# A single-core decode block with a cached attention and a gated FFN: fewer PE instructions, larger weight chunks, one store, no block

## The chip, the cores and the metric

The kernel runs on 1 core of one Trainium2 chip. Its time is the device time of one execution in microseconds (us). "The span" is what the profile covers of one execution; it is 1.2 to 2.1 us shorter than the time, and that difference will matter. The page writes PE for the matmul engine, PEld for its weight loads, DVE for the vector engine, ACT for the scalar engine, SP for the engine whose queue issues most transfers, "landing" for the arrival of a transfer, and "L575" for line 575 of the kernel that was run.

## The reference

Two tokens (batch 2, one position each) pass through an adaLN-conditioned block: attention over the last 1024 keys of a cache with 32 heads of 192, then a gated FFN.

```python
mod = (_silu(c) @ w_mod).reshape(2, 6, 1, 640)          # w_mod: 640 x 3840
h = layernorm(x) * (1 + ca) + sa
q = (h @ wq)                                             # wq: 640 x 6144
scores = einsum('bhqd,bhkd->bhqk', q, k_cache[:, :, -1024:]) * 192 ** -0.5
o = einsum('bhqk,bhkd->bhqd', softmax(scores), v_cache[:, :, -1024:])
x = x + ga * (o.reshape(2, 1, 6144) @ wo)                # wo: 6144 x 640
h = layernorm(x) * (1 + cb) + sb
x = x + gb * ((gelu(h @ w_gate) * (h @ w_up)) @ w_down)  # 640 x 1536, 640 x 1536, 1536 x 640
```

Everything is bf16. Weights and the used part of the cache are 76.9 MB, and each byte is used for two rows at most.

## The kernel before

All large loads go out from SP in the order in which they are used: w_mod, wq, then K and V of 16 groups (4 heads of one batch row, 32 partitions a head, 32 keys a partition), wo, w_gate, w_up, w_down. wq, K, V and wo pass through a ring of 8 slots.

The parts that the change touches (cuts marked):

```python
KPS = SLOT // NQ                      # wq: one k per ring slot, 5 loads
...                                   # wo: 9 tiles per slot, 6 loads
WD_SPLIT = [(0, 2), (2, 1), (3, 1)]   # w_down: 6, 3 and 3 of 12 row blocks

# scores of one group: DVE multiplies K by q (prod), PE adds up over d with an identity
o_ap = ps[:, bk, ci * JC * GC:(ci + 1) * JC * GC].rearrange("p (j c) -> p j c", c=GC)
for t in range(NCH):                  # GC = 16, NCH = 12: 12 matmuls of 256 columns
    last = e.matmul(o_ap, lhsT=ident_b[:, :], rhs=prod[:, pz, :, t * GC:(t + 1) * GC], ...)

# FFN gate and up: the weights are the stationary operand, 60 matmuls of 2 columns each
for fc in range(FC):
    a, r = divmod(fc, FR)
    for k in range(KT):
        last = e.matmul(ps[:, bk, fc * 2:fc * 2 + 2],
                        lhsT=wv[:, k, a * P * FR:(a + 1) * P * FR].rearrange("p (m r) -> p m r", r=FR)[:, :, r],
                        rhs=h2T[:, k, :], start=(k == 0), stop=(k == KT - 1))
...
# the store, two transfers, and the block that holds the engines' programs
for b in range(B):
    S.dma(("sp", "act")[b], k_dma(out[b, 0, :]..., finb[b:P:32, :]), sem_out[b], ...)
with nc.Block() as block:
    @block.sync
    def _(e):
        S.emit("sp", e, tail=sp_tail)
    ...
```

## Time and profile before

Time before: 192.12 us median of 3 runs (191.79 to 192.21).

| | before |
|---|---|
| span of the profiled run | 190.5 us |
| DMA stream | 76.9 MB, 9 tenths busy from the second to the 38th of 40 slices |
| PE, DVE busy | 57%, 47% |
| last weight piece landed | 186.8 us |
| output ready, end of the span | 188.1 us, 190.5 us |
| PE instructions (matmuls and weight loads) | 2802 |

From the page of the kernel before: its engines, the row of DMA busy tenths and the rate in 40 slices, three DMA queues (packets, MB, share of the 16 engines' time), and the start of the chain that ended last.

```profile
PE 109.4 (57%) x1401; PEld 74.3 (39%) x1401; DVE 88.7 (47%) x147; ACT 29.2 (15%) x74; POOL 3.0 (2%) x14
DMA  7999999999999999999999999999999999999960
GB/s 259 388 416 441 423 427 428 418 436 426 418 429 426 421 427 425 421 428 424 423 426 431 418 423 434 419 421 431 428 416 434 420 423 424 426 421 432 399 252 8
DMA packets 7234, 77.09 MB, mean 405 GB/s; under 512 B 818, under 2 KB 820, under 8 KB 1460
q1 hardware_dynamic: 7192, 76.88, 96.0%
q8 instruction: 11, 0.18, 0.4%
q14 instruction: 3, 0.02, 0.0%
DMA 71%; DVE 13%; SPq 5%; PE 4%; issue 3%; ACT 2%
```

The reader is to see that the DMA engines never rest before the 39th slice, and that the 39th (181.0 to 185.7 us) moves only 252 GB/s, though the last landing is yet to come: the 16 engines do not finish together. The small queue q8, "instruction", moved 11 packets of 16 KB between 26.0 and 187 us. I read them as blocks of PE's program that are fetched while the kernel runs; the experiments below show that their number goes with that of the PE instructions (9, 10 and 11 packets for 2334, 2590 and 2846).

The chain of waits of the kernel before in order of time, its last pieces (start in us, duration in us, what):

```profile
156.72 30.05 DMA r<-in_B_w_down_dram
186.77 0.04 issue
186.81 0.60 PE ps L625 x12
187.41 0.02 issue
187.44 0.33 DVE fin L630
187.77 0.02 issue
187.80 0.32 DVE finb L632
```

So the end is: a last landing at 186.77 us, 12 matmuls, two DVE instructions, then the store and the exit up to 190.5 us. The timeline of the FFN before (start, duration, engine, line, operation, operands; in brackets the idle time before and what ended it):

```profile
178.24 1.81 PE L605 MATMUL ps<-h2T,r 128*128 128x2 bf16 x60 [0.28 <-DVE h2T L376]
181.79 1.81 PE L605 MATMUL ps<-h2T,r 128*128 128x2 bf16 x60 [1.73 <-DMA r<-in_B_w_up_dram]
183.71 0.18 DVE L616 TENSOR_TENSOR aT<-ps,gl 128x24 bf16<-128x24 f32 x1 [5.53 <-PE ps L605]
```

**When each engine lands.** For each of the 49 weight and cache loads of the kernel before, all of 128 partitions, the trace records 16 increments of the load's semaphore (a counter that engines wait on), each with its time; the page counts 16 DMA engines. I read each increment as the finish of one engine. No trace shows this, as the increments don't name the engine; "an engine is late" stands below for "an increment is late". Sorted, they then show how far apart the engines are. For some transfers of the kernel before: time of the first increment, the 16 delays behind it in us, and how many packets of the instruction queue had gone before:

```
first at    delays of the 16 increments                                                    packets so far
 14.28   0.00 0.01 0.02 0.03 0.06 0.07 0.08 0.10 0.20 0.23 0.34 0.40 0.45 0.46 0.50 0.73    0
 28.99   0.00 0.04 0.05 0.06 0.09 0.10 0.12 0.13 0.25 0.36 0.43 0.47 0.48 0.52 0.74 1.78    1
 58.49   0.00 0.04 0.06 0.08 0.09 0.10 0.12 0.14 0.28 0.36 0.43 0.49 0.53 0.73 1.80 2.06    2
164.56   0.00 0.03 0.05 0.27 0.72 0.74 0.83 1.50 1.54 1.55 1.69 1.76 1.89 1.95 2.10 2.12    8
168.06   0.00 0.01 0.02 0.28 0.69 0.73 0.84 1.48 1.52 1.53 1.67 1.86 1.92 2.08 2.12 3.29    9
183.13   0.00 0.06 0.10 0.28 0.73 0.76 0.85 1.50 1.52 1.57 1.67 1.89 1.95 2.10 3.30 3.64   10
```

Packets of the instruction queue q8 started at 26.0, 56.7, 70.0, 88.4, 104.9, 121.1, 139.8, 158.1, 167.2, 181.3 and 185.9 us and took about 1.06 us each. After each of the first eight, one more engine stands about 1.5 us behind, which is more than the packet itself took (why is open), and it stays there: the DMA share is 1.01 in each of the windows from 40 to 160 us that I asked for, which leaves no idle time for catching up. One late engine of the table is not q8's: a second instruction queue, q14, moved an 8 KB packet (0.33 us) at 75.6 us, after which an engine is about 1.0 us later and stands over 1.3 us behind. So the row at 164.56 us has nine late engines after eight packets. The ninth and tenth packets of q8 make an engine late that was late already. These two engines, alone, set the landing at 186.77 us: the other fourteen had landed by 185.23.

### The profile page before, as it was taken

What the parts mean: (1) busy time and instruction counts of PE and PEld (TensorE: products, weight loads), DVE (VectorE), ACT (ScalarE), POOL (GpSimd) and SP (SyncE); (2) the same over time, 40 slices, a digit from 0 to 9 for tenths busy, and PEclk for the clock granted to TensorE, in tenths of its full rate; (3) what the DMA queues carried; (4) which work ended last, traced back from release to release, by engine and by line L of the source; (5) the groups of instructions that cost most, each with busy time, mean ns of one, the idle gap of its engine ahead of it and who ended that gap; (6) DMA issues with size and microseconds to landing.
All of it is one profiled execution on the core that took longest, in us unless ns stands there. A gap on an engine that the chain in (4) does not pass through costs nothing.

```text
span 190.5 us, 3243 instructions
## 1 busy us (share of the span) xinstructions
PE 109.4 (57%) x1401; PEld 74.3 (39%) x1401; DVE 88.7 (47%) x147; ACT 29.2 (15%) x74; POOL 3.0 (2%) x14
## 2 busy tenths in 40 slices
PE   0014853628678773674689656646759856224452
PEld 0011310105556552462457444434536624223450
DVE  6123000248699549458477476485495620003201
ACT  3031100370022101011011011012010230003400
POOL 6000000000000000000000000000000000000000
PEclk9999999999999999999957999999975995555555
DMA  7999999999999999999999999999999999999960
GB/s 259 388 416 441 423 427 428 418 436 426 418 429 426 421 427 425 421 428 424 423 426 431 418 423 434 419 421 431 428 416 434 420 423 424 426 421 432 399 252 8
DMA packets 7234, 77.09 MB, mean 405 GB/s; under 512 B 818, under 2 KB 820, under 8 KB 1460
## 3 DMA queue, kind: packets, MB, share of 16 engines
q1 hardware_dynamic: 7192, 76.88, 96.0%
q8 instruction: 11, 0.18, 0.4%
q14 instruction: 3, 0.02, 0.0%
q10 hardware_dynamic: 28, 0.01, 0.0%
HBM read 76.88 MB, written 0.00 MB: 404 GB/s over the span
## 4 chain that ended last, share of the span: by engine, by line
DMA 71%; DVE 13%; SPq 5%; PE 4%; issue 3%; ACT 2%
DMA ring<-in_A_k_cache_dram 39%; DMA ring<-in_A_wq_dram 16%; DMA r<-in_B_w_down_dram 16%; DVE prod L441 8%; SPq L246 5%; PE ps L454 3%; DVE S_sb L461 2%; ACT qbc L433 2%; PE ps L416 1%; DVE ps L436 1%; DVE M L464 1%; PE ps L480 0%; DVE rden L516 0%; PE ps L625 0%; DVE Sb_sb L486 0%
## 5 line engine op out<-in xcount | busy, mean ns | idle before, releaser
L441 DVE TENSOR_TENSOR prod<-ring,qbc 128x3072 bf16<-128x3072 bf16 x32 | 55.9, 1752 | 21.7 <-DMA ring<-in_A_k_cache_dram 21.7
L454 PE MATMUL ps<-prod,ident_b 128*128 128x256 bf16 x384 | 53.4, 296 | 21.0 <-DVE prod L441 21.0
L454 PEld LDWEIGHTS ps<-prod,ident_b 128*128 128x128 bf16 x384 | 38.2, 105 | 33.1 <-DVE prod L441 25.4
L518 ACT ACTIVATE On<-ps,rden 128x384 bf16<-128x384 f32 x16 | 9.3, 580 | 46.5 <-DVE rden L516 33.1
L480 PE MATMUL ps<-nmx,ones_f 1*128 1x4 f32 x32 | 6.5, 271 | 15.2 <-DVE nmx L471 15.2
L506 PE MATMUL ps<-ring,E_sb 128*8 128x384 bf16 x256 | 13.6, 334 | 0.0
L489 ACT ACTIVATE E_sb<-Sb_sb 128x128 bf16<-128x128 f32 x16 | 5.0, 309 | 53.3 <-DVE Sb_sb L486 53.3
L480 PEld LDWEIGHTS ps<-nmx,ones_f 1*128 1x128 f32 x32 | 5.1, 198 | 20.3 <-DVE nmx L471 20.3
L575 PE MATMUL ps<-ring,oT 128*2 128x160 bf16 x192 | 7.2, 333 | 8.3 <-DMA ring<-in_A_wo_dram 7.8
L461 DVE TENSOR_REDUCE S_sb<-ps 128x32 f32<-128x512 f32 x16 | 10.8, 673 | 1.7 <-PE ps L454 1.7
L416 PE MATMUL ps<-ring,hT 128*2 128x384 bf16 x80 | 7.1, 516 | 7.5 <-DMA ring<-in_A_wq_dram 6.7
L486 DVE TENSOR_TENSOR Sb_sb<-S_sb,ps 128x128 f32<-128x128 f32 x16 | 4.6, 288 | 10.7 <-PE ps L481 10.7
L575 PEld LDWEIGHTS ps<-ring,oT 128*2 128x2 bf16 x192 | 5.4, 115 | 9.9 <-DMA ring<-in_A_wo_dram 9.3
L592 DVE TENSOR_TENSOR lnt<-ps,modR 128x160 f32<-128x160 f32 x1 | 0.3, 324 | 17.5 <-PE ps L575 17.5
L345 PE MATMUL ps<-st,selstat 128*128 128x2 f32 x4 | 1.1, 349 | 11.2 <-ACT sqj L341 11.2
L427 DVE CAST qrow<-ps 128x384 bf16<-128x384 f32 x2 | 1.0, 553 | 13.7 <-PE ps L416 13.7
L416 PEld LDWEIGHTS ps<-ring,hT 128*2 128x2 bf16 x80 | 2.1, 108 | 12.6 <-DMA ring<-in_A_wq_dram 8.9
L530 PEld LDWEIGHTS ps<-On,zsel 128*128 128x128 bf16 x128 | 6.1, 110 | 1.2 <-ACT On L518 1.2
L530 PE MATMUL ps<-On,zsel 128*128 128x48 bf16 x128 | 6.0, 187 | 0.8 <-ACT On L518 0.8
L506 PEld LDWEIGHTS ps<-ring,E_sb 128*8 128x8 bf16 x256 | 4.9, 86 | 3.0 <-issue 0.5
L495 PEld LDWEIGHTS ps<-denp,maskc 128*128 128x128 f32 x32 | 5.3, 209 | 1.2 <-ACT E_sb L489 1.0
L396 PE MATMUL ps<-r,scT 128*2 128x480 bf16 x40 | 4.3, 596 | 2.1 <-DMA r<-in_w_mod_dram 2.1
(71 smaller groups left out, 74.9 us busy)
## 6 DMA issues: line engine op xcount, KB each, us to landing
ring<-in_A_k_cache_dram SPq DMA_DIRECT2D x16, 1536.0 KB, 25.1
ring<-in_A_v_cache_dram SPq DMA_DIRECT2D x16, 1536.0 KB, 25.6
ring<-in_A_wq_dram SPq DMA_DIRECT2D x5, 1536.0 KB, 23.9
ring<-in_A_wo_dram SPq DMA_DIRECT2D x5, 1440.0 KB, 24.7
r<-in_w_mod_dram SPq DMA_DIRECT2D x1, 4800.0 KB, 14.2
r<-in_B_w_gate_dram SPq DMA_DIRECT2D x1, 1920.0 KB, 26.9
r<-in_B_w_up_dram SPq DMA_DIRECT2D x1, 1920.0 KB, 31.0
r<-in_B_w_down_dram SPq DMA_DIRECT2D x1, 960.0 KB, 33.3
```

Of the source, the lines that this page charges most:

```text
L246: return lambda e: e.dma_start(dst, src)
L416: last = e.matmul(ps[32 * i:32 * i + B, n, 0:QW].rearrange("p (q d) -> p q d", d=Dh), lhsT=hT[:, k, :], rhs=wv[:, 2 * n:2 * n + 2, i, :], ...
L441: S.op("dve", lambda e: e.tensor_tensor(out=prod[:, 2 * (g % 2) + ci, :, :], in0=ring[:, sl, ci * JC * Dh:(ci + 1) * JC * Dh].rearrange("p ...
L454: last = e.matmul(o_ap, lhsT=ident_b[:, :], rhs=prod[:, pz, :, t * GC:(t + 1) * GC], start=(ci == 0 and t == 0), stop=(t == NCH - 1), skip ...
L461: S.op("dve", lambda e: e.tensor_reduce(out=S_sb[:, z, :], in_=ps[:, z, :].rearrange("p (j c) -> p j c", c=GC), axis=AX.X, op=ALU.add), re ...
L480: e.matmul(o_ap, lhsT=ones_f[0:1, :], rhs=nmx[:, z, :], start=True, stop=False)
L489: S.op("act", lambda e: e.activation(out=E_sb[:, z, :, :], in_=Sb_sb[:, z, :, :], func=ACTF.Exp, scale=SCALE, accum_out=denp[:, z:z + 1]), ...
L495: S.op("pe", lambda e: e.matmul(ps[:, BK_T, P + 16:P + 17], lhsT=maskc[:, :], rhs=denp[:, z:z + 1], start=True, stop=True), reads=[("denp" ...
L506: last = e.matmul(ps[32 * i:32 * i + 2 * HQ, BK_O, 0:ON], lhsT=E_sb[:, z, 2 * jp:2 * jp + 2, :].rearrange("p j h -> p (j h)"), rhs=ring[:, ...
L518: S.op("act", lambda e: e.activation(out=On[:, z, :], in_=ps[:, BK_O, 0:ON], func=ACTF.Identity, scale=rden[:, z:z + 1]), reads=[bank(BK_O ...
L530: last = e.matmul(ps[:, BK_OT, b * NT:(b + 1) * NT], lhsT=zsel[:, jj, x:x + P], rhs=On[:, z, jj * Dh + dd * NT:jj * Dh + (dd + 1) * NT], s ...
L575: last = e.matmul(ps[32 * i:32 * i + B, BK_M, 0:DR], lhsT=oT[:, t, :], rhs=wv[:, tl, i, :], start=(t == 0), stop=(t == NT - 1), tile_posit ...
```

## The change

Its stated intent: a third fewer PE instructions by wider sums and by letting the FFN weights be the moving operand, large wq and wo chunks, small last w_down pieces, one store, no block. The diff, cut to its core:

```diff
-    GC = 512 // J
+    GC = 512 // JC                       # sums: 6 matmuls of 512 columns in place of 12 of 256
-    KPS = SLOT // NQ                      # wq in 5, wo in 6 loads
-    ...
-    WD_SPLIT = [(0, 2), (2, 1), (3, 1)]
+    WQ_SPLIT = [(0, 2), (2, 3)]
+    WO_SPLIT = [(0, 28), (28, 17), (45, 3)]
+    WU_SPLIT = [(0, 3), (3, 2)]
+    WD_SPLIT = [(9, 3), (0, 5), (5, 3), (8, 1)]
...
-                e.matmul(o_ap, lhsT=ones_f[0:1, :], rhs=nmx[:, z, :], start=True, stop=False)
-                return e.matmul(o_ap, lhsT=ident_b[:, :], rhs=mneg[:, :], start=False, stop=True)
+            S.op("pe", lambda e: e.matmul(ps[:, BK_T, P:P + HQ], lhsT=bcL[:, :], rhs=bcR[:, z, :], ...
...                                        # sel: both batch rows in one matmul of 96 columns
-        def ffn_gu(bk, wv, key):           # 60 matmuls, weights stationary
+        def ffn_gu(bk, wv, name, splits):  # 20 matmuls, weights moving, four column groups
+                        wk = wv[:, k, :].rearrange("p (m i r) -> p i m r", i=NR, r=FR)
+                        for i in range(NR):
+                            last = e.matmul(ps[32 * i:32 * i + B, bk, 0:FT]..., lhsT=h2T[:, k, :],
+                                            rhs=wk[:, i, :, :], ..., tile_position=(0, 32 * i))
+        def a_T(e):                        # and 12 matmuls that transpose the result
...
-        for b in range(B):
-            S.dma(("sp", "act")[b], ...    # two stores
-        with nc.Block() as block:
-            ...
+        S.dma("sp", k_dma(out[:, 0, :].rearrange("b (i n) -> i b n", i=NR), finb[0:P:RB, :]),
+              sem_out, reads=["finb"], name="st_out")
+        S.resolve()                        # drops waits that other waits imply
+        S.emit("sp", nc.sync, tail=lambda e: e.wait_ge(sem_out, 16))
+        S.emit("pool", nc.gpsimd)
+        ...
```

The heads of a group are also no longer neighbours in memory, which lets q be read in unbroken columns of wq.

## The prediction

> **What bounds the kernel now.** The DMA stream. The page's slices show the 16 engines at 9 tenths busy from the second slice to the 38th, 416 to 441 GB/s, for 76.9 MB; PE is busy 57%, DVE 47%. The chain of waits is DMA for 71% and ends with the last w_down piece landing at 186.8 us, then 0.6 us of matmuls, 0.65 us of DVE, then 2.4 us of store and exit. So only three things count: bytes per engine, the slowest engine's finish, and what follows it. A faster PE in the attention loop is worth nothing by itself (the loop's DVE and PE wait for K).
>
> **The slowest engine.** The trace's semaphore records give 16 increments per DMA[...]. For the first loads they come within 0.73 us. For the last w_down piece: fourteen within 2.1 us of the first (183.1 to 185.2 us), two at 186.4 and 186.8 us. The instruction queue moved 11 packets of 16 KB, about 1.06 us each, and after nearly each of them one more engine is late by about 1.1 us for good. The first eight fall on different engines; the ninth (167 us) and tenth (181 us) on engines that are late already. Those two set the end. [...] 2802 PE instructions (1401 matmuls, 1401 loads) are 10.9 blocks.
>
> **What the change does.**
> - PE falls to about 1039 matmuls by my count, 2078 instructions, 8.1 blocks. Eight fetches, none doubled: last landing about 1.5 us earlier (183.1 + 2.1). This is the main gain.
> - Last w_down piece 4 matmuls instead of 12: about -0.2 us.
> - One store, no block: before, finished output to end is 2.4 us, with two stores landing at 189.8 and 190.1 us and an exit after; about -0.5 us.
> - Fewer, larger wq and wo packets (40 fewer per engine, net): rates of 12 KB and 15 KB rows differ by 0.2%, so about -0.15 us.
> - Costs off the path: queries ready about 2.3 us later (36 matmuls after the last wq landing, at 4 per 0.43 us); S reduction reads twice as much (0.67 to about 1.15 us), so DVE takes about 6.1 us a group against the stream's 7.4: it catches up by about 90 us. The ring stays issued some 10 us ahead, so no DMA gap.
> - Tail: gate and up each 5 rounds of 384 columns (about 1.65 us against 1.81), then a new transpose (12 matmuls, a copy, about 0.7 us). wo's last pieces end near 173.2 us, as before, h2T near 178.2, aT near 183.1, first down pieces done near 184.5 us, just ahead of the last landings. Little slack.
>
> **Predicted:** 192.1 - 2.5 = 189.6 us; 80% range 188.4 to 191.0. Faster by over 2%: 0.12; within 2%: 0.85; slower by over 2%: 0.03.
>
> **Right if:** the instruction queue shows 8 packets; the last landing is near 185.2 us with no engine over 2.2 us behind the first; DMA stays at 9 tenths, mean rate up about 1%; about 1.8 us from output ready to end; PE busy drops by some 20 us or more with nothing to show for it in the loop.
>
> **Wrong if:** the fetches still double up on an engine; the strided moving reads of gate and up (runs of 3 elements) run at half speed, which makes the tail compute-bound and costs 2 to 3 us; the late wq release or large wo pieces open a gap in the DMA row; or the head spread of K rows changes the rate.

The four gains in the list come to 2.35 us (1.5 + 0.2 + 0.5 + 0.15), put down as 2.5. A "block", here and in the expectations, is 256 PE instructions. The trace of the kernel before has 11 packets for 2802 PE instructions, 255 a packet, and in the experiments 256 instructions more were one packet more. That each increment is one engine's is the reading given above.

## The result

| | before | after |
|---|---|---|
| time, median | 192.06 us (191.79 to 192.21, 4 runs) | 188.92 us (188.76 to 189.1, 4 runs) |
| ratio | 1 | 0.9838, 95% interval 0.9821 to 0.9855 |
| span of the profiled run | 190.5 us | 187.6 us |
| time minus span in that run | 1.7 us | 1.3 us |
| last weight piece landed | 186.77 us | 184.75 us |
| span's end after output ready | 2.4 us | 1.8 us |

A ratio is the mean time of one kernel's runs over that of the other's of the same rounds, so it is not quite the ratio of the medians quoted. Executions over 1.5% slower than the fastest of the same kernel are left out of the means. The kernel is 1.6% faster, correct, and inside the predicted range, on its fast side.

The same lines of the page after the change:

```profile
PE 107.5 (57%) x1039; PEld 51.1 (27%) x1039; DVE 98.2 (52%) x147; ACT 29.9 (16%) x72; POOL 5.1 (3%) x23
DMA  7999998999999999999999999999999999999991
GB/s 254 402 451 435 430 459 372 422 435 424 430 422 422 427 425 426 427 424 420 419 432 432 422 423 422 421 438 422 424 423 422 419 488 428 416 384 442 398 396 45
DMA packets 6518, 77.03 MB, mean 411 GB/s; under 512 B 746, under 2 KB 876, under 8 KB 1516
q1 hardware_dynamic: 6492, 76.88, 97.1%
q8 instruction: 8, 0.13, 0.3%
q14 instruction: 2, 0.02, 0.0%
DMA 71%; DVE 15%; PE 7%; ACT 2%; SPq 2%; issue 1%
```

Bytes are the same and the DMA engines are as busy as before. The 39th slices (396 GB/s against 252) cannot be compared, as this one ends at 182.9 us, before any engine has finished; from 178.2 to 182.9 us the kernel before moved 392 GB/s too. What differs at the end is shown by the increments below. The instruction queue moved 8 packets in place of 11. PE is still busy 57%: the sums move the same columns through the array in half as many instructions (109.4 us of PE before, 107.5 after). Only the weight loads fell (74.3 to 51.1 us).

The end of the chain of waits and the FFN in the timeline, after the change:

```profile
152.72 31.64 DMA r<-in_B_w_down_dram
184.37 0.04 issue
184.41 0.72 PE ps L684 x16
185.13 0.02 issue
185.16 0.34 DVE fin L689
185.49 0.02 issue
185.52 0.32 DVE finb L691
```

```profile
175.51 1.89 PE L655 MATMUL ps<-r,h2T 128*2 128x384 bf16 x20 [0.28 <-DVE h2T L427]
180.10 0.86 PE L655 MATMUL ps<-r,h2T 128*2 128x384 bf16 x8 [0.70 <-DMA r<-in_B_w_up_dram]
181.70 0.47 PE L672 MATMUL ps<-selg,aR 128*128 128x2 bf16 x12 [0.74 <-DVE aR L664]
182.21 0.20 DVE L676 CAST aT<-ps 128x24 bf16<-128x24 f32 x1 [0.57 <-PE ps L672]
```

The gate takes as long as before (1.89 us against 1.81), the transpose and its copy take 0.7 us more, and still the tail waits for DMA. The FFN starts 2.7 us earlier than before, of which part is a higher granted clock of this run (see "The tail" below). The chain names the landing before the last one, that of the three-row piece at 184.37; the one-row piece landed at 184.75, and its matmuls are the last 4 of the 16.

The increments of the last w_down piece after the change, beside those before:

```
         first at    delays of the 16 increments
before   183.13   0.00 0.06 0.10 0.28 0.73 0.76 0.85 1.50 1.52 1.57 1.67 1.89 1.95 2.10 3.30 3.64
after    182.92   0.00 0.02 0.05 0.07 0.09 0.18 0.46 0.71 0.92 1.45 1.48 1.53 1.61 1.63 1.65 1.83
```

The first engine lands 0.21 us earlier, the last 2.02 us earlier. So nine tenths of the gain at the last landing came from the slowest engines, and one tenth from the stream's rate. Of the 8 packets, seven left an engine late; the eighth came at 182.8 us, when the first engine was about to finish.

**Two theories.** Mine: each 16 KB block of PE instructions that is fetched puts one DMA engine back for good; eight blocks fall on different engines, the ninth and tenth on engines already late; cutting PE instructions to about eight blocks takes those two away (about 1.5 us), and the rest of the gain comes from chunks, store and exit. The rival: the number of PE instructions as such is irrelevant; the larger chunks, the smaller last pieces or the lighter PE load do it, and the late engines are an accident of the run.

### The profile page after: what moved, and what is told of

Read it like the earlier page. It is cut to its first block, busy times and chain, and to the rows that moved or that the text cites. A ratio compares the mean times of both kernels' runs of the same rounds, so it can differ in the third digit from the quotient of the medians.

```text
span 187.6 us, 2409 instructions
## 1 busy us (share of the span) xinstructions
PE 107.5 (57%) x1039; PEld 51.1 (27%) x1039; DVE 98.2 (52%) x147; ACT 29.9 (16%) x72; POOL 5.1 (3%) x23
## 3 DMA queue, kind: packets, MB, share of 16 engines
q1 hardware_dynamic: 6492, 76.88, 97.1%
## 4 chain that ended last, share of the span: by engine, by line
DMA 71%; DVE 15%; PE 7%; ACT 2%; SPq 2%; issue 1%
DMA ring<-in_A_k_cache_dram 37%; DMA ring<-in_A_wq_dram 17%; DMA r<-in_B_w_down_dram 17%; DVE prod L490 9%; PE ps L502 4%; DVE S_sb L509 4%; PE ps L467 2%; SPq L266 2%; ACT qbc L483 2%; DVE ps L485 1%; DVE M L512 1%; ACT qrow L474 1%; PE ps L526 0%; DVE bcR L519 0%; PE ps L684 0%
## 5 line engine op out<-in xcount | busy, mean ns | idle before, releaser
L502 PE MATMUL ps<-prod,ident_b 128*128 128x512 bf16 x192 | 52.9, 419 | 14.4 <-DVE prod L490 14.4
L502 PEld LDWEIGHTS ps<-prod,ident_b 128*128 128x128 bf16 x192 | 17.5, 104 | 40.2 <-DVE prod L490 17.5
L509 DVE TENSOR_REDUCE S_sb<-ps 128x32 f32<-128x1024 f32 x16 | 19.3, 1206 | 2.1 <-PE ps L502 2.1
L526 PE MATMUL ps<-bcR,bcL 5*128 5x4 f32 x32 | 6.1, 258 | 21.9 <-DVE bcR L519 21.9
L467 PE MATMUL ps<-ring,hT 128*2 128x512 bf16 x60 | 6.7, 626 | 9.8 <-DMA ring<-in_A_wq_dram 8.8
L526 PEld LDWEIGHTS ps<-bcR,bcL 5*128 5x128 f32 x32 | 4.7, 183 | 26.1 <-DVE bcR L519 26.1
L622 PE MATMUL ps<-ring,oT 128*17 128x160 bf16 x192 | 5.5, 294 | 5.6 <-DMA ring<-in_A_wo_dram 5.6
L622 PEld LDWEIGHTS ps<-ring,oT 128*17 128x17 bf16 x192 | 4.9, 117 | 6.2 <-DMA ring<-in_A_wo_dram 6.2
L576 PE MATMUL ps<-On,zsel 128*128 128x96 bf16 x64 | 5.2, 241 | 0.7 <-ACT On L563 0.7
L540 PE MATMUL ps<-denp,maskc 128*128 128x1 f32 x32 | 5.1, 230 | 0.8 <-ACT E_sb L534 0.8
```

What stands on the lines that cost most here:

```text
L467: last = e.matmul(ps[32 * i:32 * i + B, n, :], lhsT=hT[:, k, :], rhs=wv[:, kk, i, n * QW:(n + 1) * QW], start=(k == 0), stop=(k == KT - 1) ...
L509: S.op("dve", lambda e: e.tensor_reduce(out=S_sb[:, z, :], in_=ps[:, 2 * z:2 * z + 2, :].rearrange("p k (j c) -> p (k j) c", c=GC), axis=A ...
L526: S.op("pe", lambda e: e.matmul(ps[:, BK_T, P:P + HQ], lhsT=bcL[:, :], rhs=bcR[:, z, :], start=True, stop=True), reads=[("bcR", z), "bcL"] ...
L540: S.op("pe", lambda e: e.matmul(ps[:, BK_T, P + 16:P + 17], lhsT=maskc[:, :], rhs=denp[:, z:z + 1], start=True, stop=True), reads=[("denp" ...
L576: last = e.matmul(ps[:, BK_OT, 0:B * NT].rearrange("p (b t) -> p b t", b=B), lhsT=zsel[:, jj, x:x + P], rhs=On[:, quad % 2, :, jj * Dh + d ...
L622: last = e.matmul(ps[32 * i:32 * i + RM, BK_M, 0:DR], lhsT=oT[:, t, :], rhs=wv[:, tl, i, :], start=(t == 0), stop=(t == NT - 1), tile_posi ...
```

## The experiments

Twelve kernels ran; the kernel before ran beside each. Its median was 192.03 to 192.06 us in each set, so times of different sets may be compared to about 0.1 us. "+" is against the changed kernel's 188.92 us. All gave correct results.

### Put PE instructions back, and nothing else: 8, 16 and 24 small matmuls a group

```diff
                 p_pv(g - 1)
                 declare_ring([("v", g - 1)])
+                def pad(e):
+                    last = None
+                    for _ in range(24):        # 8 and 16 in the other two
+                        last = e.matmul(ps[0:1, BK_M, 500:501], lhsT=ident_b[:, 0:1], rhs=ident_b[:, 0:1], start=True, stop=True)
+                    return last
+                S.op("pe", pad, reads=["ident_b"], writes=[bank(BK_M)], name="pad%d" % g)
```

The column that they write is read by nobody.

> The changed kernel plus 8 one-column matmuls per attention group (16 instructions, about 0.5 us of PE a group, into an unused PSUM column): about 2334 PE instructions, 9.1 blocks of 256. Theory (fetched blocks delay single DMA engines, the ninth hits one a second time): 9 packets on the instruction queue, one engine over 2.5 us behind the first at the last w_down piece, time +0.9 to +1.4 us on the changed kernel, unless the ninth comes too late to hit data. Rival (PE count itself does not matter; the gain is from chunks, store and exit): within 0.2 us of the changed kernel.

> The changed kernel plus 16 one-column matmuls per group, about 2590 PE instructions: 10 fetches, the ninth about 173 us, the tenth near 183 us, too late. Theory (a step when the ninth fetch still hits data): an engine about 1.2 us later than the others, 3.0 to 3.4 us behind the first, time 190.0 to 190.4 us, all of the cost of 24 per group. Rival (cost in proportion to instructions): about 189.7 us.

> The same with 24 per group: about 2846 PE instructions, as many as the kernel before: 11 packets. Theory: two or three engines doubly late, last landing 1.2 to 1.8 us later than in the changed kernel, time about 190.3 us, that is, half the gain gone though no other part of the change is undone, and not much more than with 8 per group. Rival: within 0.2 us of the changed kernel; if PE work were what counts, three times the cost of 8 per group.

| small matmuls a group | PE instructions | instruction packets at (the last ones) | late increments of the last piece | time |
|---|---|---|---|---|
| 0 | 2078 | 8: 166.4, 173.5, 182.8 us | largest delay 1.83 us | 188.92 us |
| 8 | 2334 | 9: 167.2, 173.2, 184.2 us | largest 2.06 us | 188.96 us (+0.0) |
| 16 | 2590 | 10: 166.9, 173.9, 184.3 us | 2.10, then 3.01 us | 190.07 us (+1.15) |
| 24 | 2846 | 11: 167.3, 174.7, 184.2 us | 1.94, then 3.37, 3.43 us | 190.37 us (+1.45) |

With 24 a group, the page's line of the instruction queue is as in the kernel before, although every other part of the change is in place:

```profile
q8 instruction: 11, 0.18, 0.4%
```

and the number of engines over 1.3 us behind the first counts up with the packets, then stops, and a second level appears (counted from the increments of this run):

```
landed at   packets so far   engines over 1.3 us late   of them over 2.5 us late
   15.1            0                    0                         0
   34.2            1                    1                         0
   67.5            2                    2                         0
   78.6            3                    3                         0
   93.3            4                    4                         0
  108.1            5                    5                         0
  122.8            6                    6                         0
  137.6            7                    7                         0
  152.4            8                    8                         0
  170.9            9                    8                         1
  181.4           10                    8                         2
```

This is a step, not a slope. The 256 instructions of the first pad cost nothing, since their ninth packet came at 184.2 us, when the engine that it fell on had hardly any data left (the last landing was at 184.90 us); my figure of +0.9 to +1.4 us for it missed, and the clause "unless the ninth comes too late" held. The next 256 cost 1.1 us, the next 0.3. The rival expected no cost or one in proportion. This fits eight engines that take turns, one packet each; the increments do not name the engines.

### Put PE work back without instructions

```diff
+                    for _ in range(4):
+                        last = e.matmul(ps[:, BK_M, :], lhsT=ident_b[:, :], rhs=qrow[:, 0:512], start=True, stop=True)
```

> Control: the changed kernel plus 4 matmuls of 512 columns per group, 128 instructions in all but as much PE time a group as the 24 small ones or more (about 1.3 us): about 2206 PE instructions, still 8 blocks. Theory: 8 packets, no engine over 2.2 us late, time within 0.2 us of the changed kernel. Rival (PE busy time in the loop counts): slower by as much as with 24 small ones.

Measured: 188.97 us (+0.05). PE was busy 120.9 us, 13 us more than in the changed kernel and more than with 24 small matmuls (113.9 us); 8 packets; largest delay 1.96 us.

```profile
PE 120.9 (64%) x1103; PEld 56.6 (30%) x1103; DVE 98.3 (52%) x147; ACT 29.9 (16%) x72; POOL 5.1 (3%) x23
q8 instruction: 8, 0.13, 0.3%
```

So 13 us of PE time more in this loop cost 0.05 us. What costs is the fetch: 1.15 us with two packets more.

### Cut PE instructions in the kernel before, and nothing else

```diff
-    GC = 512 // J
+    GC = 512 // JC
...
+    # gate and up: moving weights, 20 matmuls of 384 unbroken columns each, then 12 to transpose
+                for k in range(KT):
+                    for i in range(NR):
+                        last = e.matmul(ps[32 * i:32 * i + B, bk, 0:FT], lhsT=h2T[:, k, :], rhs=wv[:, k, i * FT:(i + 1) * FT], ...
```

> The kernel before with only its PE instructions cut: sums 512 columns wide and moving FFN weights with the transpose that needs, about 1141 matmuls, 2282 PE instructions, 8.9 blocks; chunks, pieces, stores, block as before. Theory: 8 packets before the last data (perhaps a ninth at the very end), last landing about 1.5 to 1.8 us earlier than before, time 190.3 to 190.8 us. Rival: within 0.3 us of the kernel before.

Measured: 191.15 us, ratio to the kernel before 0.9952 (0.9939 to 0.9964), that is 0.9 us faster. The landings did what the theory asks: largest delay of the last piece 2.16 us in place of 3.64, last landing 185.32 us in place of 186.77, which is 1.45 us earlier. (The ninth packet came at 185.1 us, too late.) The span fell by about 1.2 us, to 188.8 to 189.2 us. But the time fell by only 0.9 us, below the expected 1.3 to 1.8, because time minus span rose to 2.0 to 2.1 us from 1.8 to 1.9 in the same set. The kernel still has the block, and something outside the span takes about 0.25 us longer. No run here shows what; it stays open. So the cut of PE instructions alone is worth 0.9 us when it is added to the kernel before, and 1.45 us when it is undone in the changed kernel.

This run also compares two ways to read moving weights. Here the 384 columns are unbroken; in the changed kernel they come in runs of 3 elements, a step of 12 apart:

```profile
177.12 1.77 PE L606 MATMUL ps<-r,h2T 128*2 128x384 bf16 x20 [0.28 <-DVE h2T L378]
```

1.77 us against 1.89, both at a granted clock of 0.50: short runs cost little here, and I had named half speed as a danger.

### Undo the rest of the change, part by part

**The block back, one store:**

```diff
-        S.emit("sp", nc.sync, tail=lambda e: e.wait_ge(sem_out, 16))
-        ...
+        with nc.Block() as block:
+            @block.sync
+            def _(e):
+                S.emit("sp", e, tail=sp_tail)
+            ...
```

> The changed kernel with the block put back around the engines' programs; one store kept. Theory (the block's exit costs about 0.4 us inside the span, and time minus span, 1.3 us without and 1.75 us with it, is the block's too): 0.6 to 0.9 us slower than the changed kernel, 189.5 to 189.8 us, with the landings of the last w_down piece unmoved. Rival (the two stores cost it, not the block): within 0.2 us of the changed kernel.

Measured: 189.77 us (+0.85); last landing 184.90 us in the profiled run, 0.15 us later than in the changed kernel's. (The changed kernel with 8 small matmuls, as fast as without, also landed at 184.90 us, so 0.15 us is within what such runs scatter.) The spans of its four runs are 187.8 to 188.1 us, about 0.3 us longer than the changed kernel's (187.5 to 187.8), and time minus span is 1.8 us in each, against 1.2 to 1.3. So over half of the block's cost lies where the profile does not look. In the view of SP's waits one new wait appears at the end, for PE's sequencer:

```profile
SPq L698 <- DMA out_dram<-finb: 1.0, 1, 1.0
SPq L698 <- PEq L698: 0.2, 1, 0.2
```

**Two stores back, no block:**

```diff
-        S.dma("sp", k_dma(out[:, 0, :].rearrange("b (i n) -> i b n", i=NR), finb[0:P:RB, :]), ...
+        for b in range(B):
+            S.dma(("sp", "act")[b], k_dma(out[b, 0, :].rearrange("(i n) -> i n", i=NR), finb[b * RB:P:32, :]), sem_out[b], ...
```

> The changed kernel with the output stored by two transfers from two queues again, no block. Theory: 0.1 to 0.3 us slower than the changed kernel (the second store of before landed 0.27 us after the first). Rival: 0.6 to 0.9 us slower, and the block nothing.

Measured: 189.24 us (+0.3); time minus span is 1.2 to 1.3, as in the changed kernel. In the profiled run (189.31 us) the last landing came at 184.92 us, and from output ready to the span's end it took 2.1 us in place of 1.8. SP waits 1.3 us for the two to land, against 1.0 for one:

```profile
SPq L699 <- DMA out_dram<-finb: 1.3, 1, 1.3
```

**wq in five and wo in six loads:**

```diff
-    WQ_SPLIT = [(0, 2), (2, 3)]
-    WO_SPLIT = [(0, 28), (28, 17), (45, 3)]
+    WQ_SPLIT = [(k, 1) for k in range(5)]
+    WO_SPLIT = [(0, 9), (9, 9), (18, 9), (27, 9), (36, 9), (45, 3)]
```

> The changed kernel with wq in five pieces and wo in six again. Theory: the first engine's last landing 0.1 to 0.2 us later (32 more packets and 6 more transfers per engine), spread unchanged, time +0.1 to +0.3 us. Rival (the large chunks carry the gain): +1 us or more. The order of engines and fetches should stay: 8 packets.

Measured: 189.35 us (+0.43), 8 packets. The first engine's landing of the last piece moved from 182.92 to 183.34 us, as much as the time, so the cost is put down to the stream's rate. (The last landing moved by 0.25 us, to 185.00, in the profiled run, which at 189.12 us was the fastest of the four.) It is larger than expected, and far from the rival's 1 us. The page counts 7356 packets in place of 6492, that is 54 more for each engine and not the 32 of the expectation.

**w_down in three pieces, 12 matmuls after the last landing:**

```diff
-    WD_SPLIT = [(9, 3), (0, 5), (5, 3), (8, 1)]
+    WD_SPLIT = [(0, 6), (6, 3), (9, 3)]
```

> The changed kernel with w_down in three pieces of 6, 3 and 3 rows, in order: 12 matmuls after the last landing in place of 4. Theory: last landing unmoved within 0.1 us, end of the matmuls 0.2 to 0.3 us later, time +0.2 to +0.3 us. Rival (small last transfers land later or cost nothing): no change, or faster.

Measured: 189.10 us (+0.2, of which the interval of the ratio, 0.9835 to 0.9864 against the changed kernel's 0.9838, leaves little certain). Last landing 184.71 us, unmoved; DVE takes over at 185.19, 0.48 us later, where the changed kernel needs 0.41. In this run the 12 matmuls had a granted clock of 1.00 and took 0.39 us; in the kernel before they had 0.50 and took 0.57. The small last piece is worth 0.1 to 0.2 us at most.

Parts that no run undoes alone are the dropped waits (S.resolve), the order of heads, the single matmul for both batch rows, and the two pieces of w_up.

### What makes a large chunk cheaper: inconclusive, and a surprise

In the changed kernel, the spacing of the first engine's landings fits bytes/435 GB/s plus 0.074 us for every transfer of 128 rows (7.32 us for 3.146 MB, 10.91 us for 4.719 MB). Rows and transfers go together there, so this run was to part them:

```diff
+                if it[0] == "k":
+                    def two(e, dst=dst, src=src, sem=sem):
+                        e.dma_start(dst[0:HP, :], src[0:PH // 2]).then_inc(sem, 16)      # partitions 0 to 63
+                        return e.dma_start(dst[HP:P, :], src[PH // 2:PH])                  # partitions 64 to 127
+                    S.dma("sp", two, sem, writes=ring_key(it), name="ld_%s%d" % it, parts=2)
```

> What makes a large chunk cheaper, its fewer rows or its fewer transfers? In the changed kernel the first engine's landings fit bytes/435 GB/s plus 0.074 us for every transfer of 128 rows (K: 3.69 us for 1.573 MB; the first wo chunk: 10.62 us for 4.588 MB). Here each K load is cut in two transfers of 64 partitions: 16 transfers more, rows (packets) and bytes the same. If the cost is the transfer's: first landing of the last piece 0.6 to 1.2 us later, time 189.6 to 190.2 us. If it is the row's (8 rows an engine, about 9 ns each): within 0.2 us of the changed kernel.

Measured: 244.7 and 242.1 us, about 54.5 us slower than the changed kernel (two more runs were slow: 248.8 and 268.3 us). The engines are as busy as ever (9 tenths from the second slice to the 38th) and move far less:

```profile
GB/s 297 410 432 470 390 293 210 301 275 329 242 337 225 343 264 307 309 252 350 226 337 262 309 317 259 353 238 343 285 317 332 236 331 457 442 402 422 402 330 18
```

The low rates begin with the K loads and end with them. Sixteen extra transfers cannot cost 54.5 us at 0.07 us each. The increments show that each half is slow in itself: in the K and V loads of one group the first engine's landings are 3.36, 3.53 and 3.94 us apart (53.44, 56.97 and 60.91 us), where a whole K load of twice the bytes takes 3.69 us. A half of 0.786 MB in 3.36 to 3.53 us is 223 to 234 GB/s. That compares with 426 GB/s for a whole K load. An estimate from this one group: its K and V took 10.83 us in place of 7.38 (two loads of 3.69 us), 3.45 us more, which is 55.2 us over the 16 groups; 54.5 us were measured. So the slow halves account for nearly all of it (51.2 us), and V loads that take 0.25 us longer for the rest. Why a half is so slow is not shown, and no further run tests it. The question that the run was made for, row or transfer, stays open: the edit changed a third thing that is far larger.

### Tries at a faster version

**Fewer bytes for the late engines.** The last piece by 16 transfers of 8 partitions:

```diff
+                for j in range(16):
+                    S.dma("sp", k_dma(dst[8 * j:8 * j + 8, :], src[8 * j:8 * j + 8, :]), sem_wd[ci], writes=[("wd", ci, j)], ...
```

> Looking for a better version: the changed kernel with the last w_down piece (160 KB) loaded by 16 transfers of 8 partitions[...]. If the fetches delay the other eight, the late engines finish 0.4 us earlier: last landing about 0.3 us earlier, 188.6 us. If the fetches fall on these eight, last landing 0.3 to 0.5 us later, 189.3 us. If they fall on a mixture: later too.

Measured: 192.0 us (+3.1). The DMA engines gave 128 increments, 8 for each transfer, from 182.69 to 187.85 us. At the end they form two series (the other ends at 187.49); the later one ends at 187.23, 187.44, 187.64 and 187.85: 0.2 us from one transfer of one row of 1280 bytes to the next, where the data alone would take about 0.05 us at 27 GB/s, a sixteenth of the stream's 435 GB/s (an estimate). All three outcomes that I had written assumed no such cost. The series ends 3.0 us after the latest landing of the piece before (184.82), about 15 times 0.2 us, as if one late engine had carried a row of each of the 16 transfers; it shows no more.

**Fewer pieces, store issued by ACT:**

```diff
-    WU_SPLIT = [(0, 3), (3, 2)]
-    WD_SPLIT = [(9, 3), (0, 5), (5, 3), (8, 1)]
+    WU_SPLIT = [(0, 5)]
+    WD_SPLIT = [(0, 8), (8, 3), (11, 1)]
...
-        S.dma("sp", k_dma(out[:, 0, :]...
+        S.dma("act", k_dma(out[:, 0, :]...
```

> A try at a faster version: the changed kernel with w_up whole, w_down in three pieces of 8, 3 and 1 rows (two transfers and 16 rows per engine fewer, 0.15 us by the fit), and the store issued by ACT, whose issue took 0.57 us against 0.69 on SP. Theory: first and last landings 0.15 us earlier, store 0.1 us shorter, time 188.65 us. Rival (the matmuls after the landings become the bound with fewer pieces): no gain, or slower by up to 0.3 us.

Measured: 188.80 us (188.71 to 188.87), ratio to the kernel before 0.9831 (0.9817 to 0.9846), against 0.9838 for the changed kernel. The first landing of the last piece came 0.39 us earlier (182.53 us), but the delays of that run were larger (2.07 us), so that the last came 0.15 us earlier. This is 0.1 us better at most and not resolved. The spans were about 0.27 us shorter (187.3 to 187.4 us), but time minus span rose to 1.4 to 1.5 us from 1.3, so that part of the gain was lost outside the span; why is open. The tail was near its limit: aT was ready at 183.34 us, and PE then worked without a pause through the last pieces.

## Why the prediction was right, and where it was off

| part | predicted | measured by undoing it |
|---|---|---|
| two fetches less on late engines | 1.5 us | 1.45 us (24 small matmuls a group) |
| block and second store | 0.5 us | 0.85 + 0.3 us |
| larger wq and wo chunks | 0.15 us | 0.43 us |
| small last piece | 0.2 us | 0.2 us, barely resolved |
| sum | 2.5 us (the four make 2.35) | 3.2 us, for a gain of 3.14 us |

That the sum fits is no proof of each part: a part need not be worth the same in both kernels, as the first one shows (0.9 us when added to the kernel before).

- **What bounds the kernel:** right. DMA stayed at 9 tenths, bytes the same; 13 us of extra PE work in the loop cost nothing.
- **The slowest engine:** right in mechanism, as far as increments without names show it, and in the size of the gain. "Right if" asked for 8 packets, a last landing near 185.2 us and no engine over 2.2 us behind: 8, 184.75, 1.83. It landed 0.45 us sooner than foreseen, 0.2 us of it because the first engine was earlier. One detail was misread: a packet leaves its engine about 1.5 us behind and not 1.1. This did no harm, since the 1.5 us of gain was read from the landings of the other fourteen engines.
- **The store and exit term was mis-sized.** I read "2.4 us from output ready to the end" and took 0.5 us off it. Inside the span that was right (2.4 to 1.8 us, and I named "about 1.8"). But the page gives the span, and the time is longer: time minus span fell from 1.7 to 1.3 us when the block went, and with the block alone put back it is 1.8. That part is not in any view of the profile; only the list of times shows it. This is most of the missed 0.7 us.
- **The chunk term was mis-sized.** I compared the rates of 12 KB and 15 KB rows, "differ by 0.2%" (in the landings of the kernel before, 426.3 GB/s over 32 K and V loads and 426.9 over w_gate and w_up), and multiplied by 40 packets. By the later fit (0.074 us for 128 rows, or about 9 ns a row on an engine if each carries 8 of them) 40 rows would be 0.37 us. 0.43 was measured for undoing wq and wo, which is 6 transfers (0.44 us by the fit). A small difference of two rates was too blunt to price 40 packets.
- **PE busy "drops by some 20 us":** wrong. It fell by 1.9 us (109.4 to 107.5); what fell by 23 us was the weight loads (74.3 to 51.1). The sums still pass the same number of columns. It had no effect on the time, but it is what one gets for equating instructions with work.
- **Costs off the path:** right. The S reduction takes 1.2 us (I said 1.15), the first multiply starts about 1.9 us later (I said 2.3), DVE first waits for K again at 86.0 us (I said 90), and no gap opens in the stream: the slices of 372 and 384 GB/s fall in the large wq and wo loads, whose first landings come 10.91 and 10.62 us after those before, as the fit has it.
- **The tail:** right that it stays just ahead of the landings. wo ended near 171.2 us, not 173.2. In the window from 169 to 172 us the granted PE clock was 1.00 in place of 0.50, and 80 matmuls took 1.57 us where 48 had taken 1.77. The larger chunks are not what raised the clock: three other runs with the same wo chunks (8 small matmuls, w_down in three pieces, fewer pieces) had 0.50 there and took 2.85 us for the 80 matmuls. Nor did it matter: with 8 small matmuls the FFN started at 176.85 us, 1.3 us later than in the changed kernel, and the time was the same. So the early end was luck, and the time did not need it.

## What to carry to other kernels

Here a stream kept the DMA engines 9 tenths busy up to the 38th of 40 slices, and the end was set by two of the 16 increments of the last transfer, which came 1.20 and 1.54 us after the other fourteen. So with such a stream, look at those 16 increments, not at the mean rate. In the kernel before, each of the first eight instruction packets left one engine about 1.5 us late for good. Count PE instructions (matmuls plus weight loads) in blocks of what a packet stands for, 256 here (2334, 2590 and 2846 instructions: 9, 10 and 11 packets): fewer was worth nothing until a block that doubled up disappeared, and then about a microsecond (1.1 us from 16 to 8 small matmuls a group). And compare the time with the span: of the 0.85 us that the block cost, over half was in neither the span nor any view of the profile.
